# Seven plain chunks and twenty pairs instead of nine and nineteen, with two thirds of the weight sums behind the transforms

## The chip, the cores and the metric

The kernel runs on one core of one Trainium2 chip. The metric is the device time of one execution in microseconds (us). Engines are written as in the profile: PE is TensorE (PEld its weight loads), DVE is VectorE, ACT is ScalarE, POOL is GpSimd, SP is SyncE, which here only issues DMAs.

## What is computed

```python
X = np.fft.rfft(x, axis=1)                 # x: 8 x 3008 x 256
Yr = Xr @ w_r - Xi @ w_i + b_r
Yi = Xr @ w_i + Xi @ w_r + b_i
Y = sign(Y) * maximum(abs(Y) - 0.01, 0)    # on Yr and Yi, the soft threshold
y = np.fft.irfft(Y, n=3008, axis=1)        # 24064 tokens of 256
gate = 1 / (1 + exp(-(y @ w_gate)))        # 256 x 1536
out = (gate * (y @ w_val)) @ w_out         # 1536 x 256
```

Everything is float32. A product of the FFN (and of the mixing by w_r, w_i) is made of three matmuls on rounded high and low parts of its operands, so that a float32 result comes out of the faster matmul type.

## The kernel before

The transforms go batch by batch: a small DFT over 47 (`fwd_d`), a DFT over 64 (`fwd_b`), the complex mixing with the soft threshold (`mix`, 84 calls for batches 1 to 7), and the way back (`inv_b`, then `inv_a`). Between these steps the data go out to HBM and come back. Batch 0 is transformed first, alone. Everything else runs beside the FFN.

The FFN has two forms. **Plain chunks** are 512 tokens wide (`CW`), and there are `NPL` = 9 of them. Each has 12 units `ffn[j]`; a unit is `ffn1` (12 matmuls of 512 columns, a sigmoid, a product, a split into high and low) and `ffn2` of two units earlier (6 matmuls). **Pairs** are 1024 tokens wide, `NPR` = 19 of them; they use a seven-product scheme on 2x2 blocks for both layers, 378 matmuls of 512 columns where two plain chunks have 432. The pairs need sums of weight blocks: `make_t` makes those of the first layer (12 calls, into the DRAM tensor `td`), `make_s` those of the second (6 calls, into `sd`). Both run on POOL and store by POOL's own DMA queue.

Order of work: units 0 to 11 run with the last of the front work. The transforms of batches 1 to 7 are a list `side` of steps with weights; the loop over `j` (units 12 on) issues a unit and then as many steps as the weight per unit allows, such that all but the steps of the last group's inverse (`behind_last`, one `inv_a` a unit) are gone at unit `part`, the last 20 units (`LAST_GAP`) remaining. So in the program before 76 units (12 to 87) lie beside the transforms, then come 20 units with the 16 `inv_a` of the last group, then the pairs. When the transforms are through, their pools are closed and the pool `p4` of the pairs' weights and operands is opened on their memory. A scheduler places the instructions of all these streams on each engine's queue, in an order that is fixed when the program is built.

In the program before, the sums are issued one at each third unit from unit 34 on, all beside the transforms, in buffers that the transforms use too. SP issues nearly all loads and stores in one queue: the loads `vf<-vd` of `inv_a` (two buffers), its stores `yd<-yf`, and, as early as the scheduler finds place for them, the pairs' first weight loads `w1s<-td` and `w2s<-sd` (rings of `NW1` = 4 and `NW2` = 3 buffers in `p4`).

In the pairs the order is written by a planner (`arrange`) with a table of nudges (`NUDGE`); the table, the planner's costs and the pairs' tasks are the same in both programs.

Of the kernel before, what the change touches and what calls it, by code (L numbers as in the profile page):

```python
# [22 lines left out]
LAM = float(np.float32(0.01))  # L23
GROUPS = (1, 1, 2, 2, 2)
CW = 512
NPL = 9
HW = 512
FG = 3
RING, L1_BANKS, L2_BANKS = 6, 3, 2

NF2K, NR2K, NLD, NST, NBIG, NMF, NME, NVF, NVO, NHH, NSG, NYF, NYT = 5, 4, 3, 3, 5, 3, 2, 2, 1, 3, 2, 3, 3
NCB, NTMP, NW1, NW2, NOP = 9, 17, 4, 3, 3
# [208 lines left out]
def tile_fft_mix_ffn(ctx: ExitStack, tc, x, w_r, w_i, b_r, b_i, w_one, w_out, mf, mi, mis, fa, ft, out):  # L241
    nc = tc.nc

    B, D, S = x.shape[0], w_r.shape[0], R1 * R2
    P = 128
    XR = x.shape[2]
    CT = D // P
    NF = w_one.shape[0]
# [7 lines left out]
    NH = NF // 2  # L256
# [23 lines left out]
    def f2k(name):  # L280
        return p2.tile([P, 2, D], F32, tag="f2k", bufs=NF2K, name=name)
# [21 lines left out]
    def big(name):  # L303
        return p2.tile([P, 4, D], F32, tag="big", bufs=NBIG, name=name)
# [126 lines left out]
        held["xs", b, q] = xh, xl  # L431


    def soft(s):
        c = f2k("yc")
        nc.vector.tensor_scalar(c, s, -LAM, LAM, op0=ALU.max, op1=ALU.min)
        sub(c, s, c)  # L437
        return c

    def mix(b, q):  # L440
        xh, xl = held.pop(("xs", b, q))
        pm = bank("pm")
# [12 lines left out]
        c = soft(s)
        yh = r2k("yh")
        yl = r2k("yl")
        nc.scalar.copy(yh, c)  # L458
        sub(yl, c, yh)
        held["ys", b, q] = yh, yl  # L460
# [82 lines left out]
    def result(name):  # L543
        return p3.tile([P, CW], F32, tag="ry", bufs=NYF, name=name)
# [152 lines left out]

    def make_t(fp, i):  # L700
        f0, f1 = 2 * fp, 2 * fp + 1
        g = nc.gpsimd
        b = p2.tile([P, 2, D], F32, tag="st", bufs=NST, name="tb").rearrange("p a (b n) -> p a b n", b=2)
        t = result("tt").rearrange("p (a b n) -> p a b n", a=2, b=2)
        for k, f in enumerate((f0, f1)):
            g.tensor_add(b[:, k], w1h[:, f, i], w1l[:, f, i])
        t = t.rearrange("p a b n -> p (a b) n")
        g.tensor_sub(t[:, 0], b[:, 1, 0], b[:, 0, 0])
        g.tensor_sub(t[:, 2], b[:, 1, 1], b[:, 1, 0])
        g.tensor_add(t[:, 1], t[:, 2], b[:, 0, 0])  # L710
        g.tensor_sub(t[:, 3], b[:, 0, 1], t[:, 1])
        r = p2.tile([P, 4, 2, P], F32R, tag="big", bufs=NBIG, name="tr")
        for k in (0, 2):
            g.tensor_copy(r[:, k:k + 2, 0], t[:, k:k + 2])
            g.tensor_sub(r[:, k:k + 2, 1], t[:, k:k + 2], r[:, k:k + 2, 0])
        g.dma_start(td[fp, i][:, 3:], r.bitcast(F32))
        for v, w in enumerate((w1h, w1l)):
            g.dma_start(td[fp, i][:, 0:2, v], w[:, f0, i].bitcast(F32))
            g.dma_start(td[fp, i][:, 2, v], w[:, f1, i, 1].bitcast(F32))

    def make_s(fp):
        g = nc.gpsimd
        if fp >= NH - FG:
            g.dma_start(pd[fp - NH + FG], w2[:, 2 * fp:2 * fp + 2].bitcast(F32))
        a = p2.tile([P, 2, D], F32, tag="st", bufs=NST, name="sa")
        g.tensor_add(a, w2[:, 2 * fp:2 * fp + 2, 0], w2[:, 2 * fp:2 * fp + 2, 1])
        a11, a21, a12, a22 = a[:, 0, :P], a[:, 0, P:], a[:, 1, :P], a[:, 1, P:]
        w = big("sw").rearrange("p a n -> p (a n)").rearrange("p (k n) -> p k n", n=P)
        zero = w[:, 7]
        g.memset(zero, 0.0)  # L730
        g.tensor_copy(w[:, 0], a11)
        g.tensor_sub(w[:, 1], zero, a12)
        g.tensor_sub(w[:, 3], zero, a22)
        g.tensor_add(w[:, 4], a22, a21)
        g.tensor_sub(w[:, 5], w[:, 4], a11)
        g.tensor_sub(w[:, 6], a11, a21)
        g.tensor_sub(w[:, 2], a12, w[:, 5])
        for k0, k1 in ((0, 4), (4, 7)):
            r = p2.tile([P, 4, 2, P], F32R, tag="big", bufs=NBIG, name="sr")[:, :k1 - k0]
            g.tensor_copy(r[:, :, 0], w[:, k0:k1])  # L740
            g.tensor_sub(r[:, :, 1], w[:, k0:k1], r[:, :, 0])
            g.dma_start(sd[fp // FG, k0:k1, :, fp % FG].rearrange("k p v n -> p k v n"), r.bitcast(F32))
# [22 lines left out]
    def first_operands():  # L765

        y = held["y", 0]
        a11, a21, a12, a22 = y[:, 0, 0], y[:, 0, 1], y[:, 1, 0], y[:, 1, 1]
        s1, s2 = (p4.tile([P, HW], F32, tag=f"{n}0", bufs=1, name=n) for n in ("s1f", "s2f"))
        g = nc.gpsimd  # L770

        def split(name, v):
            t = xs[name] = xop(name)
            nc.scalar.copy(t[:, 0], v)
            sub(t[:, 1], v, t[:, 0])

# [12 lines left out]
        return [sums, lambda: split("s2", s2), lambda: split("a12", a12), lambda: split("s1", s1), s3,
                lambda: split("a22", a22), s4]  # L790
# [702 lines left out]
```

## Time and profile before

| | us |
|---|---|
| median of 3 runs (2697.5 to 2703.36) | 2700.75 |
| the profiled execution, its own time | 2710.75 |
| its span, first to last instruction | 2708.9 |
| units 12 to 87 beside the transforms, from 183.5 to 912.2 | 728.7 |
| the last 20 units, from 912.2 to 1021.2 | 109.0 |
| the 19 pairs, from 1021.2 on | 1687.7 |

Times in the profile are microseconds from the start of the span. Busy times of PE are modelled: matmuls overlap, so the mean time of one matmul (0.39 us) is longer than the step from one to the next. An engine's queue is served in order. A wait that the profile shows on a queue (SPq, POOLq) holds back everything behind it in that queue.

### The profile page before, as it was taken

Reading aid. Unit: us, or ns where it says so; the run is one execution under the profiler, and the core shown is the slowest. Engines: PE = TensorE matmul, PEld = TensorE weight load, DVE = VectorE, ACT = ScalarE, POOL = GpSimd, SP = SyncE. Lnnn points to the kernel's source line nnn. Section 1 sums busy time; section 2 is a strip of 40 time slices with the busy share of each in tenths; the row PEclk is TensorE's granted clock in tenths of the full one; section 3 lists DMA queues with packets and bytes.
Section 4 is the critical chain, followed back from the end, with each engine's and each line's share of the span. In section 5 each row is a group of like instructions: output and inputs, shape, how many; then the busy total and the mean of one; then the engine's idle time right before and its main releaser. Section 6 shows DMA issues by size and latency. Waiting matters only on the chain.

```text
span 2708.9 us, 45080 instructions
## 1 busy us (share of the span) xinstructions
PE 2662.7 (98%) x16763; PEld 2178.5 (80%) x16763; DVE 2140.7 (79%) x3100; ACT 1670.5 (62%) x2852; POOL 1055.0 (39%) x963
## 2 busy tenths in 40 slices
PE   9999999999999999999999999999999999999999
PEld 6778888888888878878788788878788788887877
DVE  5778888687789537888888888888888788888876
ACT  4565554545444446676677766766667667776665
POOL 1441012132235013544555445444554455544532
PEclk9999999999999999999999999999999999999999
DMA  9987655677666675878877888787877788787874
GB/s 294 293 285 197 193 151 168 204 208 208 179 185 179 171 218 164 251 237 251 263 238 246 251 246 265 236 247 237 256 249 242 234 269 239 244 259 243 259 227 135
DMA packets 257659, 617.82 MB, mean 228 GB/s; under 512 B 26464, under 2 KB 130656, under 8 KB 257440
## 3 DMA queue, kind: packets, MB, share of 16 engines
q1 hardware_dynamic: 222720, 521.29, 58.5%
q0 software_dynamic: 34608, 93.60, 16.2%
q8 instruction: 133, 2.18, 0.3%
q14 instruction: 86, 0.70, 0.1%
q10 hardware_dynamic: 112, 0.04, 0.0%
HBM read 440.50 MB, written 116.13 MB: 205 GB/s over the span
## 4 chain that ended last, share of the span: by engine, by line
PE 62%; DMA 14%; DVE 10%; ACT 6%; POOL 4%; issue 3%; SPq 0%; DVEq 0%; POOLq 0%; ACTq 0%
PE z L1155 15%; PE l2z L1155 13%; DMA h<-h 11%; PE c L1155 7%; PE pm L447 4%; PE b L1155 3%; PE pb L413 2%; POOL t L1320 2%; PE pia L524 2%; PE pg L577 2%; ACT op L1331 1%; PE pg L578 1%; POOL h L1320 1%; PE po L605 1%; PE pv L577 1%
## 5 line engine op out<-in xcount | busy, mean ns | idle before, releaser
L1155 PE MATMUL z<-xop,w1s 128*128 128x512 f32 x2592 | 684.3, 391 | 11.4 <-ACT tmp L1246 11.1
L1155 PE MATMUL l2z<-op,w2s 128*128 128x512 f32 x2331 | 599.8, 392 | 3.9 <-DMA w2s<-sd 1.9
L1155 PEld LDWEIGHTS z<-xop,w1s 128*128 128x128 f32 x2592 | 484.9, 188 | 123.8 <-ACT tmp L1246 24.0
L1155 PEld LDWEIGHTS l2z<-op,w2s 128*128 128x128 f32 x2331 | 436.2, 188 | 108.2 <-ACT tmp L1351 7.4
L1246 ACT COPY tmp<-z 128x512 f32<-128x512 f32 x684 | 394.3, 584 | 183.1 <-PE z L1155 175.2
L1333 DVE TENSOR_TENSOR op<-h,op 128x1024 fp32r<-128x1024 f32 (+1 forms) x444 | 472.2, 1078 | 24.9 <-ACT op L1331 19.5
L1331 ACT CAST op<-h 128x1024 fp32r<-128x1024 f32 (+1 forms) x444 | 366.4, 837 | 176.1 <-DMA h<-h 100.1
L1155 PE MATMUL c<-xop,w1s 128*128 128x512 f32 x1296 | 362.1, 392 | 5.1 <-DVE h L1287 3.3
L1293 POOL TENSOR_TENSOR h<-tmp 128x512 f32<-128x512 f32 x114 | 180.1, 1580 | 379.6 <-DVE tmp L1249 362.6
L1155 PEld LDWEIGHTS c<-xop,w1s 128*128 128x128 f32 x1296 | 242.7, 188 | 62.8 <-DVE h L1287 10.5
L1249 DVE TENSOR_TENSOR tmp<-tmp,c 128x512 f32<-128x512 f32 x342 | 231.5, 681 | 62.9 <-ACT tmp L1246 41.2
L1320 POOL TENSOR_TENSOR t<-h 128x512 f32<-128x512 f32 x111 | 173.3, 1562 | 158.0 <-DVE h L1285 158.0
L1265 ACT ACTIVATE tmp<-tmp 128x512 f32<-128x512 f32 x342 | 210.3, 632 | 28.4 <-DVE tmp L1249 28.4
L1314 POOL DMA_DIRECT2D h<-h x148 | 128.3, 900 | 165.8 <-DVE h L1289 56.0
L447 PE MATMUL pm<-w_sb,xsh 128*128 128x256 f32 x1008 | 184.4, 285 | 0.0
L1155 PE MATMUL b<-xop,w1s 128*128 128x512 f32 x648 | 182.3, 390 | 0.0
L447 PEld LDWEIGHTS pm<-w_sb,xsh 128*128 128x128 f32 x1008 | 152.9, 189 | 1.0 <-ACT xsh L429 0.4
L1320 POOL TENSOR_TENSOR h<-h 128x512 f32<-128x512 f32 x111 | 148.9, 1341 | 8.7
L458 ACT CAST yh<-yc 128x512 fp32r<-128x512 f32 x84 | 52.2, 621 | 147.0 <-DVE yc L437 146.9
L1155 PEld LDWEIGHTS b<-xop,w1s 128*128 128x128 f32 x648 | 121.3, 188 | 26.0 <-DVE tmp L1249 0.5
L447 PE MATMUL pm<-w_sb,xsl 128*128 128x256 f32 x504 | 139.6, 277 | 0.0
L585 DVE TENSOR_TENSOR sg<-sg,pv 128x512 f32<-128x512 f32 x108 | 74.1, 686 | 74.2 <-PE pv L579 56.0
(199 smaller groups left out, 4933.0 us busy)
## 6 DMA issues: line engine op xcount, KB each, us to landing
w1s<-td SPq DMA_DIRECT2D x228, 896.0 KB, 6.3
w2s<-sd SPq DMA_DIRECT2D x259, 384.0 KB, 4.3
h<-h POOLq DMA_DIRECT2D x74, 512.0 KB, 6.2
zf<-zd SPq DMA_DIRECT2D x96, 256.0 KB, 3.5
vf<-vd SPq DMA_DIRECT2D x128, 192.0 KB, 4.0
vd<-vz SPq DMA_DIRECT2D x84, 256.0 KB, 2.7
ypair<-yd SPq DMA_DIRECT2D x19, 1024.0 KB, 7.4
out_dram<-acc SPq DMA_DIRECT2D x76, 256.0 KB, 4.3
```

The source lines that it names most:

```text
L447: nc.tensor.matmul(o, l, r, start=(i == 0), stop=(i == len(mms) - 1))
L577: nc.tensor.matmul(t, wh, yth[:, ct], start=(ct == 0), stop=False)
L585: nc.vector.tensor_mul(h, sg, pv)
L1155: nc.tensor.matmul(o, ws[i], vs[j], start=first and not i and not j, stop=i == 1, skip_group_check=not first)
L1246: return t, on("ACT", 0.59, at, lambda: a_.copy(t.get(), z.get()), [z], [t], deps)
L1249: return on("DVE", 0.67, at, lambda: add(t.get(), s.get(), o.get()), [x for x in (s, o) if x is not t], [t], deps)
L1265: return on("ACT", 0.635, at, lambda: a_.activation(t.get(), (o or t).get(), AF.Sigmoid), [o] if o else [], [t], deps)
L1293: made[3, q] = on("POOL", 1.3, 16, lambda: g_.tensor_mul(at_h(3), g22.get(), v.get()), [g22, v], [h], [d22, e22], True)
L1314: return [[on("POOL", 0.9, at + q0, lambda q0=q0, q1=q1: g_.dma_start(h.get()[:, dst, q0:q1], h.get()[:, src, q0:q1], accum_op=ALU.add), [ ...
L1320: return [[on("POOL", 1.3, at + q, lambda q=q: g_.tensor_sub(v()[:, q], h.get()[:, a, q], h.get()[:, b, q]), [h], [o], sum((d[q] for d in ...
L1331: hi = on("ACT", 0.19 + 0.43 * n, at - 8 + q0, lambda q0=q0, q1=q1: a_.copy(t.get()[:, 0, q0:q1], v()[:, q0:q1]), [t_in], [t], sum((d[i] f ...
L1333: lo.append([on("DVE", 0.13 + 0.555 * n, at - 5 + q0, lambda q0=q0, q1=q1: sub(t.get()[:, 1, q0:q1], v()[:, q0:q1], t.get()[:, 0, q0:q1]), ...
```

## The change

- `NPL` goes from 9 to 7, and with it the pairs from 19 to 20. The number of units falls from 108 to 84; units 12 to 63 (52 of them) now carry the same transforms, and the last 20 are units 64 to 83.
- `LATE` = 12: of the 18 sums, six `make_t` are issued beside the transforms, one at each sixth unit. The other six `make_t` and all six `make_s` are issued after the transforms, two a unit from unit 64 on, in `p4`: the sums themselves in the fourth buffer of the ring `w1s` (`room`), their rounded parts in the three buffers of the ring `w2s` (`rounded`).
- The stores of the unsummed weights move out of `make_t` and `make_s` into `store_plain`, one at each third unit from unit 24 on. `make_s` rounds and stores in three pieces instead of two, `make_t` (the late ones) stores in two pieces instead of one.
- `soft`: for odd `q` (42 of 84 calls) the threshold is `min(s + LAM, relu(s - LAM))`, a Relu on ACT and one DVE instruction, instead of two DVE instructions.
- The four sums of the first pair's operands (`first_operands`) move from POOL to DVE.

```diff
-NPL = 9
+NPL = 7
+LATE = 12
 ...
-    def soft(s):
+    def soft(s, by_act=False):
         c = f2k("yc")
+        if by_act:
+            nc.scalar.activation(c, s, AF.Relu, bias=lam)
+            nc.vector.scalar_tensor_tensor(c, s, LAM, c, op0=ALU.add, op1=ALU.min)
+            return c
         nc.vector.tensor_scalar(c, s, -LAM, LAM, op0=ALU.max, op1=ALU.min)
         sub(c, s, c)
 ...
-        c = soft(s)
+        c = soft(s, q % 2 == 1)
 ...
+    def room():
+        return p4.tile([P, 14 * P], F32, tag="w1s3", bufs=1, name="sums")
+    def rounded(n):
+        turns[0] += 1
+        return p4.tile([P, FG, 2, P], F32R, tag=f"w2s{turns[0] % NW2}", bufs=1, name="hilo")[:, :n]
 ...
-        for k0, k1 in ((0, 4), (4, 7)):
-            r = p2.tile([P, 4, 2, P], F32R, tag="big", bufs=NBIG, name="sr")[:, :k1 - k0]
+        for k0, k1 in ((0, 3), (3, 6), (6, 7)):
+            r = rounded(k1 - k0)
 ...
-        g = nc.gpsimd
+        g = nc.vector          # first_operands
 ...
-        if sums and j > 3 * NF - 3 and j % 3 == 1:
+        if len(sums) > LATE and j >= 2 * NF and j % 6 == 0:
+            sums.pop(0)()
+        if plain and j >= 2 * NF and j % 3 == 0:
+            plain.pop(0)()
+        for _ in range(2 if p4 and sums else 0):
             sums.pop(0)()
```

Three places show what becomes of the queues. Line numbers of the changed program are its own (L501 before is L507 there, L536 is L542, L1342 is L1375). A bracket names the semaphores that an instruction waits for: DMASW is a DMA issued by POOL, DMAHW one issued by SP, the others are engines.

The first place is SP's queue in the last 20 units, around the first load of second-layer weights for the pairs (`w2s<-sd`). Before:

```order
L536 DMA yd_104<-yf_12250 128x2x188 [waits DMAHW5_49,Activation_49]
L501 DMA vf_12280<-vd7_99 48x1024 [waits DMAHW6_49,PE_49]
L501 DMA vf_12280<-vd7_99 48x1024 [waits DMAHW7_49]
L1342 DMA w2s_13007<-sd_102 128x768 [waits DMAHW0_49]
L536 DMA yd_104<-yf_12317 128x2x188 [waits DMAHW1_49,Activation_49]
L536 DMA yd_104<-yf_12320 128x2x188 [waits DMAHW2_49,Activation_49]
L501 DMA vf_12358<-vd7_99 48x1024 [waits DMAHW3_49,PE_49]
L501 DMA vf_12358<-vd7_99 48x1024 [waits DMAHW4_49]
```

And in the changed program:

```order
L507 DMA vf_11788<-vd7_99 48x1024 [waits DMAHW7_49,DMAHW0_49,PE_49]
L542 DMA yd_104<-yf_11753 128x2x188 [waits Activation_49]
L542 DMA yd_104<-yf_11756 128x2x188 [waits DMAHW1_49,Activation_49]
L507 DMA vf_11788<-vd7_99 48x1024 [waits DMAHW2_49]
L1375 DMA w2s_12365<-sd_102 128x768 [waits DMASW5_49,DMASW6_49,DMASW4_49,DMASW7_49,DMASW2_49,DMAHW3_49,DMASW1_49,Pool_49]
L1231 DMA ypair_12367<-yd_104 128x2x1024 [waits DMAHW4_49]
L542 DMA yd_104<-yf_11825 128x2x188 [waits DMAHW5_49,Activation_49]
L542 DMA yd_104<-yf_11828 128x2x188 [waits DMAHW6_49,Activation_49]
L507 DMA vf_11860<-vd7_99 48x1024 [waits DMAHW7_49,PE_49]
L507 DMA vf_11860<-vd7_99 48x1024 [waits DMAHW0_49]
```

The load now waits for POOL and for six of POOL's stores, the last of which is that of `hilo_11416`, a part of the last `make_s`. Behind it in the queue stand the loads of the last five `inv_a` (vf_11860 and four more) and the stores of their results.

The second place is POOL's queue where the sums end and the pairs begin. Before, the last `make_s` stands beside the transforms:

```order
L740 CAST sr_11232<-sw_11219 128x3x128
L741 TENSOR_TENSOR sr_11228<-sw_11219,sr_11228 128x4x128 [waits Pool_49]
L741 TENSOR_TENSOR sr_11232<-sw_11219,sr_11232 128x3x128 [waits Pool_49]
L742 DMA sd_102<-sr_11228 128x4x256 [waits Pool_49]
L742 DMA sd_102<-sr_11232 128x3x256 [waits Pool_49]
L778 TENSOR_TENSOR s1f_12545<-ypair_12323 128x512 [waits DMAHW7_49,DMASW2_49]
```

In the changed program, the end of the last sum (ahead of it stand the eleven other late sums, without other work between them):

```order
L766 CAST hilo_11420<-sums_11406 128x3x128 [waits DMASW1_49]
L766 CAST hilo_11416<-sums_11406 128x3x128 [waits DMASW2_49,Pool_49]
L767 TENSOR_TENSOR hilo_11420<-sums_11406,hilo_11420 128x3x128 [waits Pool_49]
L767 TENSOR_TENSOR hilo_11416<-sums_11406,hilo_11416 128x3x128 [waits Pool_49]
L768 DMA sd_102<-hilo_11420 128x3x256 [waits Pool_49]
L768 DMA sd_102<-hilo_11416 128x3x256 [waits Pool_49]
L766 CAST hilo_11424<-sums_11406 128x128 [waits DMASW3_49]
L767 TENSOR_TENSOR hilo_11424<-sums_11406,hilo_11424 128x128 [waits Pool_49]
L768 DMA sd_102<-hilo_11424 128x256 [waits Pool_49]
L1244 TENSOR_TENSOR s1f_12411<-ypair_12367 128x512 [waits DMAHW4_49,DMAHW0_49,DVE_49]
```

The last `make_s` now ends right ahead of the pairs' first POOL instruction. The first late sum (not shown) waits for DVE's last soft threshold of an odd q and for the last mixing matmuls; from there the twelve follow each other on POOL without a break.

The third place is DVE's queue around a soft threshold (`ys` is its input, `yc` its result). Before:

```order
L453 TENSOR_TENSOR ys<-pm_5383,yt 64x256
L454 TENSOR_TENSOR ys<-yt 64x256
L436 TENSOR_SCALAR yc<-ys 128x512
L437 TENSOR_TENSOR yc<-ys,yc 128x512
L585 TENSOR_TENSOR sg<-sg,pv 128x512
```

In the changed program, for an odd q:

```order
L459 TENSOR_TENSOR ys<-pm_5610,yt 64x256
L460 TENSOR_TENSOR ys<-yt 64x256
L440 SCALAR_TENSOR_TENSOR yc<-ys,yc 128x512
L428 TENSOR_TENSOR xsf<-xsf 128x2x128
L455 TENSOR_TENSOR yt<-pm,bias_sb 128x512
```

One instruction has gone, and the one that is left stands right behind the sum that ACT's Relu reads. It is so in 21 of the 42 places; in the other 21 one or two other DVE instructions stand between.

## Rows read from the trace of the kernel before

**Rows 1.** The page's first part: busy time, share of the span and count.
```profile
PE 2662.7 (98%) x16763; PEld 2178.5 (80%) x16763; DVE 2140.7 (79%) x3100; ACT 1670.5 (62%) x2852; POOL 1055.0 (39%) x963
```

**Rows 2.** Busy times by stage: front and units 0 to 11, units 12 to 87 beside the transforms, the last 20 units, the pairs. Columns: stretch, length, busy us (and count) of PE, PEld, DVE, ACT, POOL, granted PE clock, DMA share, GB/s.
```profile
0.00:183.50 183.50, 172.86 (x984) 124.21 (x985) 123.19 (x213) 102.32 (x186) 61.82 (x104) 0.98 0.95 304
183.50:912.20 728.70, 719.61 (x7055) 619.26 (x7055) 602.27 (x1020) 366.88 (x648) 171.78 (x245) 0.99 0.63 184
912.20:1021.20 109.00, 107.06 (x1534) 86.06 (x1526) 36.25 (x50) 45.37 (x89) 7.19 (x5) 0.98 0.71 201
1021.20:2708.90 1687.70, 1663.20 (x7210) 1348.97 (x7208) 1378.99 (x1818) 1155.96 (x1930) 814.22 (x609) 1.00 0.78 240
```

**Rows 3.** The same columns for three stretches beside the transforms, each of 12 mixings.
```profile
290.70:382.50 91.80, 91.80 (x730) 79.44 (x730) 80.14 (x146) 48.80 (x84) 5.39 (x9) 1.00 0.56 158
602.10:720.30 118.20, 117.68 (x1380) 101.05 (x1379) 90.51 (x151) 60.25 (x110) 31.72 (x50) 1.00 0.69 201
818.10:912.20 94.10, 91.77 (x1091) 81.93 (x1092) 84.23 (x136) 43.20 (x79) 35.40 (x44) 1.00 0.55 164
```

**Rows 4.** PE in the last 20 units, in order of time: start, us, instruction, in brackets the idle time before it and what ended it. The second to the eighteenth matmul of a unit, then two parts of one `inv_a` and the next unit.
```profile
982.70 0.40 PE L578 MATMUL pg<-ytl,w1h 128*128 128x512 f32 x1
...
986.34 0.39 PE L607 MATMUL po<-hl,w 128*128 128x512 f32 x1
986.83 0.28 PE L524 MATMUL pia<-ft_sb,vf 48*64 48x47 f32 x2
987.52 1.14 PE L524 MATMUL pia<-ft_sb,vf 48*64 48x47 f32 x62 [0.41 <-DMA vf<-vd]
```

**Rows 5.** One instruction that each pair but the first has once, on POOL: min/median/max ns, first and last start.
```profile
L1216 POOL TENSOR_TENSOR ypair<-ypair x18: 1294/1736/1747, 1026.9 to 2522.4; 128x512 f32<-128x512 f32 x18
```

**Rows 6.** DVE's groups by line beside the transforms (183.5 to 912.2): count, busy us, mean ns of one, idle time before them and what ended it.
```profile
L437 DVE TENSOR_TENSOR yc<-ys,yc 128x512 f32<-128x512 f32 x83 | 62.8, 757 | 2.5
L459 DVE TENSOR_TENSOR yl<-yc,yh 128x512 fp32r<-128x512 f32 x83 | 61.7, 743 | 21.6 <-ACT yh L458 16.5 <-PE pv L579 4.8
L594 DVE TENSOR_TENSOR hl<-sg,hh 128x512 fp32r<-128x512 f32 x77 | 58.3, 757 | 23.2 <-ACT hh L593 22.3
...
L585 DVE TENSOR_TENSOR sg<-sg,pv 128x512 f32<-128x512 f32 x76 | 52.3, 688 | 16.0 <-ACT sg L583 7.5 <-PE pv L579 6.6
L436 DVE TENSOR_SCALAR yc<-ys 128x512 f32<-128x512 f32 x84 | 41.1, 490 | 2.2
```

**Rows 7.** Two groups of the pairs, same columns, over the whole span: the nearest to ACT's Relu and to DVE's new instruction.
```profile
L1265 ACT ACTIVATE tmp<-tmp 128x512 f32<-128x512 f32 x342 | 210.3, 632 | 28.4 <-DVE tmp L1249 28.4
L1287 DVE SCALAR_TENSOR_TENSOR h<-c,tmp 128x512 f32<-128x512 f32 x111 | 76.4, 689 | 2.6
```

**Rows 8.** POOL in order of time: the first and last instruction of a quick and of an ordinary `make_t`, then of a quick and of a slow `make_s`.
```profile
709.70 1.41 POOL L706 TENSOR_TENSOR tb<-w1h,w1l 128x256 f32<-128x256 f32 x2 [35.52 <-DMA vd<-vz]
711.19 0.46 POOL L708 TENSOR_TENSOR tt<-tb 128x128 f32<-128x128 f32 x1
...
716.30 0.57 POOL L716 DMA_DIRECT2D td<-tr  x1 [0.15 <-issue]
...
432.27 1.59 POOL L706 TENSOR_TENSOR tb<-w1h,w1l 128x256 f32<-128x256 f32 x2 [21.42 <-DMA vd<-vz]
...
439.65 0.57 POOL L716 DMA_DIRECT2D td<-tr  x1 [0.31 <-POOL tr L715]
...
782.81 1.44 POOL L726 TENSOR_TENSOR sa<-w 128x512 f32<-128x512 f32 x1 [15.61 <-DMA vd<-vz]
...
792.21 1.54 POOL L742 DMA_DIRECT2D sd<-sr  x2
...
817.81 1.38 POOL L726 TENSOR_TENSOR sa<-w 128x512 f32<-128x512 f32 x1 [23.84 <-DMA vd<-vz]
...
829.26 1.53 POOL L742 DMA_DIRECT2D sd<-sr  x2
```

**Rows 9.** SP's queue in the last 20 units, in order of time.
```profile
964.93 0.92 SPq L501 DMA_DIRECT2D vf<-vd  x2
965.91 0.42 SPq L1342 DMA_DIRECT2D w2s<-sd  x1
```

**Rows 10.** DMA issues: what, queue, count, KB each, median us from issue to landing. The first two are of the last 20 units, the third of the whole span.
```profile
vf<-vd SPq DMA_DIRECT2D x34, 192.0 KB, 4.2
...
w2s<-sd SPq DMA_DIRECT2D x3, 384.0 KB, 4.6
...
sd<-sr POOLq DMA_DIRECT2D x6, 384.0 KB, 5.1
```

**Rows 11.** First and last start of three instructions (min/median/max ns, first and last start): DVE's two last soft thresholds; the `inv_a` matmuls of the last 20 units (starts come in groups some 5.4 us apart); the first product of the pairs.
```profile
L437 DVE TENSOR_TENSOR yc<-ys,yc x2: 691/692/693, 905.1 to 912.2; 128x512 f32<-128x512 f32 x2
...
L524 PE MATMUL pia<-ft_sb,vf x1152: 223/232/253, 919.4 to 1010.0; 48*64 48x47 f32 x192
...
L1155 PE MATMUL c<-s,w1s x72: 389/389/434, 1021.2 to 1102.5; 128*128 128x512 f32 x72
```

**Rows 12.** Before the first plain unit PE waits for a DMA: the wait, and the stages around it (columns as in rows 2; the eighth number is the granted PE clock).
```profile
103.12 2.24 PE L524 MATMUL pia<-ft_sb,vf 48*64 48x47 f32 x64 [3.17 <-DMA vf<-vd]
...
98.00:102.30 4.30, 1.95 (x5) 0.49 (x3) 2.44 (x4) 2.78 (x6) 2.73 (x6) 1.00 0.91 240
102.30:109.10 6.80, 5.98 (x121) 4.97 (x125) 1.01 (x2) 0.85 (x2) 3.41 (x7) 0.50 1.02 370
```

More of the change, by code (lines that the diff above doesn't have):

```diff
@@ L688, in ffn_units, with store_plain @@
         return [lambda n=n: unit(n) for n in range(len(seq))], own(0), own(NPL - 1)[-1] + 1
+    def room():
+        return p4.tile([P, 14 * P], F32, tag="w1s3", bufs=1, name="sums")
+    turns = [0]
+    def rounded(n):
+        turns[0] += 1
+        return p4.tile([P, FG, 2, P], F32R, tag=f"w2s{turns[0] % NW2}", bufs=1, name="hilo")[:, :n]
+    def store_plain(fp, i):
+        for v, w in enumerate((w1h, w1l)):
+            nc.gpsimd.dma_start(td[fp, i][:, 0:2, v], w[:, 2 * fp, i].bitcast(F32))
+            nc.gpsimd.dma_start(td[fp, i][:, 2, v], w[:, 2 * fp + 1, i, 1].bitcast(F32))
+        if i and fp >= NH - FG:
+            nc.gpsimd.dma_start(pd[fp - NH + FG], w2[:, 2 * fp:2 * fp + 2].bitcast(F32))
     def make_t(fp, i):
@@ L702, in make_t @@
         g = nc.gpsimd
-        b = p2.tile([P, 2, D], F32, tag="st", bufs=NST, name="tb").rearrange("p a (b n) -> p a b n", b=2)
-        t = result("tt").rearrange("p (a b n) -> p a b n", a=2, b=2)
+        if p4:
+            b, t = (room_[:, 4 * P * k:4 * P * (k + 1)].rearrange("p (a b n) -> p a b n", a=2, b=2)
+                    for room_ in (room(),) for k in range(2))
+        else:
+            b = p2.tile([P, 2, D], F32, tag="st", bufs=NST, name="tb").rearrange("p a (b n) -> p a b n", b=2)
+            t = result("tt").rearrange("p (a b n) -> p a b n", a=2, b=2)
         for k, f in enumerate((f0, f1)):
@@ L711, in make_t @@
         g.tensor_sub(t[:, 3], b[:, 0, 1], t[:, 1])
-        r = p2.tile([P, 4, 2, P], F32R, tag="big", bufs=NBIG, name="tr")
+        r = None if p4 else p2.tile([P, 4, 2, P], F32R, tag="big", bufs=NBIG, name="tr")
         for k in (0, 2):
[L714 to L719, printed above, removed]
+            o = rounded(2) if p4 else r[:, k:k + 2]
+            g.tensor_copy(o[:, :, 0], t[:, k:k + 2])
+            g.tensor_sub(o[:, :, 1], t[:, k:k + 2], o[:, :, 0])
+            if p4:
+                g.dma_start(td[fp, i][:, 3 + k:5 + k], o.bitcast(F32))
+        if r is not None:
+            g.dma_start(td[fp, i][:, 3:], r.bitcast(F32))
     def make_s(fp):
         g = nc.gpsimd
-        if fp >= NH - FG:
-            g.dma_start(pd[fp - NH + FG], w2[:, 2 * fp:2 * fp + 2].bitcast(F32))
-        a = p2.tile([P, 2, D], F32, tag="st", bufs=NST, name="sa")
+        v = room()
+        a = v[:, 8 * P:12 * P].rearrange("p (f n) -> p f n", f=2)
         g.tensor_add(a, w2[:, 2 * fp:2 * fp + 2, 0], w2[:, 2 * fp:2 * fp + 2, 1])
         a11, a21, a12, a22 = a[:, 0, :P], a[:, 0, P:], a[:, 1, :P], a[:, 1, P:]
-        w = big("sw").rearrange("p a n -> p (a n)").rearrange("p (k n) -> p k n", n=P)
+        w = v[:, :8 * P].rearrange("p (k n) -> p k n", n=P)
         zero = w[:, 7]
@@ L803, in tile_fft_mix_ffn @@
     bias4 = p0.tile([P, D], F32, name="bias4")
-    ebias = cw.tile([P, P], F32, name="ebias")[:, :1]
+    ebias = cw.tile([P, P], F32, name="ebias")
+    ebias, lam = ebias[:, :1], ebias[:, 1:2]
     ft_sb = const.tile([P, P], F32, name="ft_sb")
@@ L904, in tile_fft_mix_ffn @@
     nc.vector.memset(ebias, -896.0 * 2.0 ** 23)
+    nc.vector.memset(lam, -LAM)
     mfs, mis_ = {}, {}
@@ L1048, in tile_fft_mix_ffn @@
     p4 = None
+    plain = [lambda fp=fp, i=i: store_plain(fp, i) for fp in range(NH) for i in range(2)]
     sums = [lambda fp=fp, i=i: make_t(fp, i) for fp in range(NH) for i in range(2)] + [lambda fp=fp: make_s(fp) for fp in range(NH)]
```

## The prediction

> **What bounds the kernel now.** I read four views, from the whole to the place. The page's busy times come first: PE 98% of the span, DVE 79% [rows 1]. Such a share hides stages, so the second view is the busy time by stage [rows 2]. Beside the transforms PE is busy for 719.6 of 728.7 us, DVE for 602.3, POOL for 171.8; in the last 20 units DVE has 36.3 of 109.0 and POOL next to nothing; in the pairs PE has 1663 of 1688. So PE sets the pace in all three, and POOL and DVE lie idle in the last 20 units. The third view cuts the transforms' stage finer [rows 3]: the stretches from 290.7 and from 818.1 have DVE at 80.1 of 91.8 and 84.2 of 94.1 us, almost the second bound. Fourth come the queues in the last 20 units. The reader should see in [rows 4] that an inverse step waits 0.41 us for its load vf<-vd, which has come only just in time, and in [rows 9] that the pairs' first w2s load is issued at 965.9, between the loads and stores of the inverse steps, 55 us before the pairs begin at 1021.2 [rows 11]. Before, that is free: it waits for nothing that is late.
>
> **The change part by part.**
>
> *One more pair.* One instruction a pair starts 18 times from 1026.9 to 2522.4 [rows 5]: 1495.5 / 17 = 88.0 us a pair. Its order, its table and its loads are unchanged, so **+88.0**.
>
> *24 plain units less.* Seventeen instructions of a unit, the second to the eighteenth, start from 982.70 to 986.34 [rows 4]: 3.64 / 16 = 0.2275 us a matmul, 18 of them 4.10 us. As long as PE is the bound beside the transforms, 52 units instead of 76 save 24 x 4.10 = 98.3 us there; the transforms' own matmuls stay. But the transforms' DVE work stays too and is pressed into less time. DVE's work falls by 24 x (0.688 + 0.757) = 34.7 us with the units [rows 6]. A soft threshold costs DVE 0.490 + 0.757 us before [rows 6]; the one instruction after I take from the nearest row, 0.689 [rows 7]. That is 0.56 less, 42 times: 23.4 us. With two thirds of the sums gone from POOL there, DVE gets quicker: the threshold's second instruction takes 0.757 on average, but 0.692 at the end of the stage, where POOL stands still [rows 6, 11]. Three such instructions (L437, L459, L594) have about 0.065 us each to gain, 243 times [rows 6], 15.8 us; two thirds of that are 10. DVE is left with 602 - 35 - 23 - 10 = 534 us for 630, 85% against 83% before. On average PE stays the bound. In the two close stretches DVE had 164.4 of 185.9 us, 88% [rows 3]. They lose 24 x 185.9 / 728.7 = 6.1 units, 25 us of PE's work and 9 of DVE's; the 12 cheaper ones of their 24 thresholds give back 7, and the missing sums some 2. PE would then need 161 us, DVE 146 at the 88% that it reached, 166. That costs 5 us; with a part of the next item I take **-90** in all, and -98 as one end.
>
> *The wait in the cheaper threshold.* ACT's Relu costs 0.632 [rows 7], 42 times 26.5 us on an engine that is busy 367 of 729 [rows 2]: hidden. DVE has to wait for it, and in 21 places with nothing between: 21 x 0.7 (0.632 and a hop) = 15 us of idle time at most, which eats most of the 23 saved. If none of it hides and DVE sets the pace, the other end is -98 + 5 + 15 = -78. Less than nothing it cannot cost, and since DVE had 126 us of idle time in this stage [rows 2], I have put only 3 into the -90.
>
> *Six sums and the plain stores beside the transforms.* These are what POOL did there before, at a slower rate. POOL is busy 172 of 729 us [rows 2]: 0.
>
> *First pair's sums on DVE.* Four instructions of about 0.7 us in a stretch where DVE is busy a third of the time [rows 2]: 0.
>
> *Twelve sums in the last 20 units.* This is the term that decides. POOL is free there, so the sums themselves cost nothing. But their buffers are w2s and w1s3, and SP's first w2s load must wait for the store of the last sum. Behind it in SP's queue stand the loads of the last five inverse steps, and PE cannot pass these. How long do the sums take? A quick `make_t` took 709.70 to 716.87, 7.2 us, an ordinary one 432.27 to 440.22, 8.0; a quick `make_s` 782.81 to 793.75, 10.9, a slow one 817.81 to 830.79, 13.0 [rows 8]. A late `make_t` has one DMA issue more (0.57), a late `make_s` a third piece: one more issue (0.77) and the fixed part of two instructions. Two sizes give that part: 0.46 us for 128 columns and 1.41 / 2 for 256 [rows 8], so 0.22 each. That makes 7.7 to 8.5 and 12.1 to 14.2: twelve sums take 119 to 136 us. All these were measured beside a DVE that was busy for 80 to 90% of the time [rows 3]; in the last units it is busy for a third. If POOL loses beside DVE the share that DVE loses beside POOL (0.692 / 0.757 = 0.91), 119 becomes 109. I take **114**, with 109 and 136 as ends.
>
> The sums start at about the end of the last threshold, 912.9 on the clock of before [rows 11]. The fifth inverse step from the end began at 986.8 [rows 4], 73.9 us later, the last ended at 1010. With the change its load comes after 114 us of sums, 5.1 for the landing of the last store, 2.5 for six issues of 0.42 us on SP, and 4.2 for its own landing [rows 9, 10]: 125.8. So PE stands for 125.8 - 73.9 = **+52**, with 47 and 74 as ends. Nothing covers it: the units behind the step are in PE's queue behind it, and the 34.4 us from there to the pairs come after. The pairs' own loads are late by no more, so nothing is added then.
>
> *PE's clock.* After a wait of 3.17 us PE ran at a granted clock of 0.50 for 6.8 us, the lower of its two levels, 1.2 GHz [rows 12]. A wait of 50 us should do the same once: half of 6.8 is lost at most, **+2**.
>
> Sum: 88 - 90 + 52 + 2 = **+52 us**. The profiled execution took 2710.75 itself (its span 2708.9); it lies 10 us above the median of the runs, 2700.75, to which I add the difference: **2753**.
>
> A rule on the sums' length: the Trainium skill's page SBUF — State Buffer, section "SBUF: two separate sides", says that a VectorE instruction with two SBUF inputs and a GpSimd one that reads SBUF lock each other out for a whole instruction. The rows agree in kind (0.757 against 0.692), and by the rule the late sums would also wait out what DVE does in their first 74 us.
>
> **The rivals.**
>
> 1. *The sums wait for DVE.* DVE is busy 36.3 of 109 us in the last units [rows 2], so 24.6 in the 74 us before PE stops. If POOL stood still in all of that, on top of the 119 of the quick rows, the sums would take 144, and PE would stand for 82: 2753 + 30 = 2783. For it speaks the spread of one kind of sum from 10.9 to 13.0 us; against it that a part of DVE's work reads PSUM and that the 119 hold such waits already.
>
> 2. *DVE becomes the bound beside the transforms.* The wait for ACT takes all that the threshold saves, and the close stretches follow DVE: the stage shrinks by 75 instead of 90, and the time is 2768. For it speaks that the new instruction stands right behind its input in half of the places; against it, that PE kept 91.8 of 91.8 us beside a DVE at 87% [rows 3].
>
> 3. *Faster: SP's queue never stands.* If the last store has landed when SP reaches the load, the term of 52 and the clock's 2 are gone and the rest is 88 - 90, with 98 instead of 90 even -10: 2691 to 2701, in the middle 2698. It decides at the sums' length: to be done in 73.9 - 5.1 - 2.5 - 4.2 = 62 us, a sum would have to take 5.2 on average, where no `make_t` took under 7.1 and no `make_s` under 10.9. It could also be that the change doesn't do what it seems to, if the wait named in the queue were met by an earlier store; but the load writes a buffer that the last sum rounds into.
>
> **How the numbers follow.** Main case 0.65 (2753, by its ends 2753 - 8 - 5 = 2740 to 2753 + 12 + 22 = 2787), first rival 0.12, second 0.13, third 0.10. The range leaves out the third rival, and at the top the case that both far ends meet; below 2740 it keeps 6 us for what the rows don't tell: **2734 to 2785**. A measurement of this kernel can tell 0.2%, 5.4 us, from no change. Half of the third rival's times, 2691 to 2701, lie more than that below 2700.75: faster 0.05, same 0.05, and **slower 0.90**, all other cases.
>
> **What would show it.** In the profile of the changed kernel: the stage beside the transforms ends some 90 us earlier; on SP a wait of about 50 us ahead of the w2s load and none of it before; an idle time of PE ahead of an inverse step (pia), ended by the load vf<-vd, of 47 to 74 us; POOL without a gap from the last threshold on for 109 to 136 us; then 34 us to the pairs, 88 us a pair. It is wrong if PE has no such gap, if POOL's sums are through within 62 us, or if DVE rather than PE is without idle time beside the transforms.

## The result and the profile after

The change makes the kernel slower: 2737.8 us, median of 4 runs (2734.39 to 2740.26), against 2701.07 for the kernel before beside it (2697.5 to 2703.36); ratio 1.0135, 95% interval 1.0119 to 1.0151. The profiled execution took 2734.39 us, span 2732.6.

Of the page after, from the busy times in 40 slices of 68 us (tenths) the rows of PE and POOL, and the granted clock:
```profile
PE   9999999999999399999999999999999999999999
...
POOL 1431111010109525445544455545554455444532
PEclk9999999999999699999999999999999999999999
```
The fourteenth slice is the only one in which PE stands for most of the time, and its granted clock is lower there. The rows by stage (cut after the last soft threshold and at the first pair; columns as in [rows 2]) say what moved:
```profile
0.00:183.50 183.50, 173.34 (x985) 124.36 (x986) 123.74 (x214) 103.08 (x186) 61.67 (x104) 0.98 0.95 305
183.50:817.00 633.50, 620.29 (x6626) 538.97 (x6625) 516.95 (x923) 363.72 (x640) 63.39 (x89) 1.00 0.69 199
817.00:976.10 159.10, 109.31 (x1513) 88.42 (x1513) 40.52 (x53) 44.08 (x87) 105.23 (x181) 0.83 0.62 190
976.10:2732.60 1756.50, 1739.55 (x7588) 1420.21 (x7586) 1449.10 (x1914) 1216.91 (x2032) 858.15 (x642) 1.00 0.79 243
```
Against [rows 2] the stretch beside the transforms is 95.2 us shorter, the last 20 units are 50.1 longer, the pairs 68.8 longer: +23.7, and so much lie the two profiled spans apart. (The medians lie 36.7 apart; on the pairs more below.) In the third row PE's busy time has hardly grown: the 50 us are a stop.

PE in that stage, in order of time (start, us, instruction, the idle time before it and what ended it):
```profile
893.75 0.39 PE L613 MATMUL po<-hl,w 128*128 128x512 f32 x1
939.98 0.41 PE L530 MATMUL pia<-ft_sb,vf 48*64 48x47 f32 x2 [45.84 <-DMA vf<-vd]
```
The releaser is a load. Whether that load was slow or late is not in this row; it is in SP's queue, in order of time:
```profile
883.83 0.47 SPq L507 DMA_DIRECT2D vf<-vd  x1
930.90 0.34 SPq L1375 DMA_DIRECT2D w2s<-sd  x1
931.29 0.43 SPq L1231 DMA_DIRECT2D ypair<-yd  x1
931.82 0.92 SPq L542 DMA_DIRECT2D yd<-yf  x2
932.84 1.04 SPq L507 DMA_DIRECT2D vf<-vd  x2
```
and in what SP waited for over the stage (us in total, times, longest):
```profile
SPq L1375 <- DMA sd<-hilo: 46.3, 1, 46.3
```
SP stood for 46.3 us at the w2s load, for the store of a late sum, and issued the next load of an inverse step 49 us after the one before. POOL's queue shows the sums that it waited for, the first instruction of the first one, the first of each `make_s`, and the last store:
```profile
817.79 1.86 POOL L732 TENSOR_TENSOR sums<-w1h,w1l 128x256 f32<-128x256 f32 x2 [122.12 <-DVE yc L440]
...
866.32 1.28 POOL L752 TENSOR_TENSOR sums<-w 128x512 f32<-128x512 f32 x1
...
877.61 1.29 POOL L752 TENSOR_TENSOR sums<-w 128x512 f32<-128x512 f32 x1
...
888.40 1.28 POOL L752 TENSOR_TENSOR sums<-w 128x512 f32<-128x512 f32 x1
...
899.00 1.27 POOL L752 TENSOR_TENSOR sums<-w 128x512 f32<-128x512 f32 x1
...
909.19 1.27 POOL L752 TENSOR_TENSOR sums<-w 128x512 f32<-128x512 f32 x1
...
919.37 1.27 POOL L752 TENSOR_TENSOR sums<-w 128x512 f32<-128x512 f32 x1
...
928.97 0.58 POOL L768 DMA_DIRECT2D sd<-hilo  x1 [0.30 <-POOL hilo L767]
```
The twelve sums run from 817.79 to 929.55, 111.8 us, without a wait of more than 2.0 us. They answer to [rows 8].

### The profile page after: what moved, and what is told of

It is laid out like the page before. It is cut to its first block, busy times and chain, and to the rows that moved or that the text cites. A ratio compares the mean times of both kernels' runs of the same rounds, so it can differ in the third digit from the quotient of the medians.

```text
span 2732.6 us, 45175 instructions
## 1 busy us (share of the span) xinstructions
PE 2642.5 (97%) x16709; PEld 2172.0 (79%) x16709; DVE 2130.3 (78%) x3102; ACT 1727.8 (63%) x2944; POOL 1088.4 (40%) x1016
## 4 chain that ended last, share of the span: by engine, by line
PE 68%; DVE 9%; DMA 8%; POOL 7%; ACT 5%; issue 2%; SPq 0%; POOLq 0%; DVEq 0%; ACTq 0%
PE z L1188 18%; PE l2z L1188 16%; PE c L1188 9%; DMA h<-h 6%; PE pm L453 4%; PE b L1188 4%; PE pb L414 2%; POOL t L1353 2%; ACT op L1364 1%; PE pia L530 1%; PE pa L314 1%; PE pg L583 1%; DVE op L1366 1%; PE po L611 1%; PE po L612 1%
## 5 line engine op out<-in xcount | busy, mean ns | idle before, releaser
L1188 PE MATMUL z<-xop,w1s 128*128 128x512 f32 x2736 | 720.3, 391 | 5.8 <-ACT tmp L1279 5.7
L1188 PE MATMUL l2z<-op,w2s 128*128 128x512 f32 x2457 | 627.1, 390 | 1.4 <-DMA w2s<-sd 1.1
L1188 PEld LDWEIGHTS z<-xop,w1s 128*128 128x128 f32 x2736 | 512.3, 188 | 120.7 <-ACT tmp L1279 15.3
L1188 PEld LDWEIGHTS l2z<-op,w2s 128*128 128x128 f32 x2457 | 459.6, 188 | 104.2 <-ACT tmp L1384 3.5
L1279 ACT COPY tmp<-z 128x512 f32<-128x512 f32 x720 | 415.8, 585 | 191.1 <-PE z L1188 183.5
L1366 DVE TENSOR_TENSOR op<-h,op 128x1024 fp32r<-128x1024 f32 (+1 forms) x468 | 496.4, 1075 | 23.4 <-ACT op L1364 17.2
L1364 ACT CAST op<-h 128x1024 fp32r<-128x1024 f32 (+1 forms) x468 | 386.3, 838 | 168.3 <-DMA h<-h 91.1
L1188 PE MATMUL c<-xop,w1s 128*128 128x512 f32 x1368 | 381.8, 392 | 5.3 <-DVE h L1320 3.6
L1188 PEld LDWEIGHTS c<-xop,w1s 128*128 128x128 f32 x1368 | 256.1, 188 | 65.9 <-DVE h L1320 11.2
L732 POOL TENSOR_TENSOR tb<-w1h,w1l 128x256 f32<-128x256 f32 x12 | 11.3, 956 | 360.6 <-DMA vd<-vz 257.0
L591 DVE TENSOR_TENSOR sg<-sg,pv 128x512 f32<-128x512 f32 x84 | 57.7, 687 | 124.4 <-ACT sg L589 70.1
```

Of the source, the lines that this page charges most:

```text
L591: nc.vector.tensor_mul(h, sg, pv)
L1188: nc.tensor.matmul(o, ws[i], vs[j], start=first and not i and not j, stop=i == 1, skip_group_check=not first)
L1279: return t, on("ACT", 0.59, at, lambda: a_.copy(t.get(), z.get()), [z], [t], deps)
L1364: hi = on("ACT", 0.19 + 0.43 * n, at - 8 + q0, lambda q0=q0, q1=q1: a_.copy(t.get()[:, 0, q0:q1], v()[:, q0:q1]), [t_in], [t], sum((d[i] f ...
L1366: lo.append([on("DVE", 0.13 + 0.555 * n, at - 5 + q0, lambda q0=q0, q1=q1: sub(t.get()[:, 1, q0:q1], v()[:, q0:q1], t.get()[:, 0, q0:q1]), ...
```

## The experiments

The theory: SP's first load for the pairs waits for the last sum, and the loads of the inverse steps wait behind it in the same queue. The rivals: the inverse steps wait for POOL, for the sums' bytes or for the clock; or the time is lost to DVE.

**1. Six late sums instead of twelve.**
```diff
-LATE = 12
+LATE = 6
-        if len(sums) > LATE and j >= 2 * NF and j % 6 == 0:
+        if len(sums) > LATE and j >= 2 * NF and j % 3 == 0:
```


> The changed kernel with six of the twelve late sums put back beside the transforms (all make_t there, at each third unit of the last two thirds; only the six make_s behind it). Theory of the queue (SP's first w2s load waits for the last late sum, the loads of five inverse steps wait behind it): six make_s take about 63 us instead of 111.8, so the last sum ends about 880 and SP comes free before PE wants what stands behind; the PE gap of 45.8 us shrinks to 0 to 5 us, six more sums beside the transforms cost 0 to 6 us there; 2690 to 2700 us, faster than the kernel before. Rival (the sums' place costs by contention with DVE or by the clock, and the gap has another cause): the gap stays above 30 us and the time above 2720 us.

Measured: 2734.07 us, ratio to before 1.011 (1.0086 to 1.0134): a miss for the time, and for the gap, which shrank to 14.8 us where 0 to 5 were expected:
```profile
PE pia L530 <- DMA vf<-vd: 15.5, 3, 14.8
```
The six `make_s` took 67.8 us, 846.2 to 914.0, 5 more than expected. But the stretch beside the transforms, here to 845.0, grew:
```profile
183.50:845.00 661.50, 637.82 (x6620) 546.81 (x6619) 523.85 (x921) 362.38 (x638) 103.66 (x154) 0.98 0.67 195
```
That is 28 us more than the 633.5 above for the same matmuls: 10.5 of it idle time of PE (661.50 - 637.82 against 13.2), 17.5 busy time, at a granted clock of 0.98 instead of 1.00. The waits of PE that a DMA ended grew from 1.7 to 8.9 us. One place, around an inverse step and a wait for zf<-zd:
```profile
660.00:665.00 5.00, 3.34 (x72) 2.34 (x71) 2.61 (x5) 2.83 (x6) 1.57 (x2) 0.85 0.59 185
665.00:670.00 5.00, 5.00 (x16) 4.13 (x16) 0.00 (x0) 0.96 (x2) 0.00 (x0) 0.50 0.94 262
670.00:675.00 5.00, 1.22 (x9) 0.91 (x7) 1.65 (x2) 1.42 (x2) 4.19 (x8) 0.84 1.06 250
675.00:680.00 5.00, 4.79 (x15) 4.19 (x16) 1.19 (x2) 1.56 (x3) 1.01 (x2) 0.50 1.05 295
```
After each short stop (660 to 665, 670 to 675) PE runs at a granted clock of 0.50, the lower of its two levels, for some microseconds. Only the place of six sums differs, so what the smaller gap gave (the last units are 29.6 us shorter) was paid there. What of a sum delays the loads was not separated; the DMA engines are full (0.94 to 1.06) in the last three of these rows.

**2. Twelve late sums, and the loads that wait for them in POOL's queue.**
```diff
-            ins = [on("SP", 0.45, at - 16, lambda: nc.sync.dma_start(w.get().bitcast(F32), sd[gi, r]), [], [w], lat=1.25)]
+            ins = [on("SP", 0.45, at - 16, lambda: (g_ if g == 0 and r in FIRST else nc.sync).dma_start(w.get().bitcast(F32), sd[gi, r]), [], [w], lat=1.25)]
...
-                           lambda: nc.sync.dma_start(t.get().bitcast(F32), td[k // 2 % NH, k % 2]), writes=[t], lat=2.7)
+                           lambda: (g_ if k == NW1 - 1 else nc.sync).dma_start(t.get().bitcast(F32), td[k // 2 % NH, k % 2]), writes=[t], lat=2.7)
```
(FIRST = (0, 1, 4).)

> The changed kernel with the sums where they are, but the loads that wait for a late sum (the first three w2s loads and the last w1s load) issued from GpSimd's queue behind the sums instead of from SyncE's. Theory of the queue: SP never stands, the loads of the inverse steps land in time, the PE gap of 45.8 us ahead of pia goes and the dip of the clock with it; 2737.8 - 45.8 - 2.3 = about 2690 us (2686 to 2696). Rival (inverse steps wait for the bytes of the sums, or for GpSimd, and not for the queue): a gap of 30 us or more stays and the time stays above 2720 us.

Measured: 2688.73 us, 0.9937 (0.9918 to 0.9955) of before, so it beats both kernels. PE's longest wait for vf is 0.7 us, and the stage has 114.2 us instead of 159.1, with the sums as long as ever (POOL 105.5):
```profile
PE pia L531 <- DMA vf<-vd: 1.6, 3, 0.7
...
820.00:934.20 114.20, 110.70 (x1515) 89.43 (x1514) 40.02 (x53) 44.61 (x88) 105.51 (x179) 0.94 0.76 241
```
Same sums, same bytes, other queue, no stop: the theory holds and the first rival is out. The dip of the clock did not go with the stop, though that was expected: the stage's granted clock is 0.94, where the kernel before has 0.98.

**3. Only the w2s loads moved** (the first of the two edits of experiment 2).

> As the kernel with four loads moved, but only the three w2s loads leave SyncE's queue; the w1s load that reads the last late sum stays there, about two inverse steps (10.9 us) later in SP's order. Theory of the queue: any one load in it that waits for the last sum is enough to hold what stands behind; the gap of 45.8 us shrinks by the work that is now ahead of the stop, to about 35 us, and the time is about 2727 us. Rival (only the w2s loads hold): about 2690 us, as with four loads moved.

Measured: 2727.35 us, 1.0085 (1.0065 to 1.0105). PE's waits for loads in that stage, and SP's:
```profile
PE pia L531 <- DMA vf<-vd: 39.5, 7, 35.5
```
```profile
SPq L1221 <- POOL hilo L768: 38.2, 1, 38.2
```
The gap is 35.5 us as expected: one waiting load is enough, and what counts is how much work stands ahead of it in the queue: PE comes to the stop 11.1 us later (one inverse step further) and goes on only 0.8 later.

**4. Experiment 2 with every threshold on DVE.**
```diff
-        c = soft(s, q % 2 == 1)
+        c = soft(s)
```


> As the kernel with four loads moved, with the soft threshold of every mix on VectorE alone, as in the kernel before. It prices the ScalarE half of the threshold without the gap. The forecast took +0 to 15 us for ScalarE's Relu on the path; the stretch beside the transforms came out at 633.5 us, 5 us less than forecast, with TensorE busy 620.3 of it, so the threshold there should be worth little: 2688 to 2698 us (0 to 8 us slower than with it, as VectorE gets some 0.5 us more for each of the odd mixes). Rival (VectorE bounds the stretch once 24 units are gone): 2705 us or more.

Measured: 2691.02 us, 0.9949 (0.993 to 0.9969), against 0.9937 with it. The stage ends 2.6 us later (822.6 against 820.0); DVE is busy 536.8 of 639.1 us there instead of 518.4 of 636.5. By the medians the threshold is worth 2.3 us, which the intervals do not tell from nothing. DVE's 18.4 us of added work cost the stretch 2.6 us, so DVE was not the bound.

**5. The chunks alone.**
```diff
-NPL = 9
+NPL = 7
-        if sums and j > 3 * NF - 3 and j % 3 == 1:
+        if sums and j >= 2 * NF and j % 2 == 0:
```


> The kernel before with only the number of plain chunks changed (seven and twenty pairs); all eighteen sums stay beside the transforms, at each second unit from the 24th on, and the threshold stays on VectorE. It asks whether the late sums are needed for the shorter stretch. One pair adds 87 to 88 us; 24 units less take 80 to 98 us from the stretch beside the transforms. If TensorE still sets the pace there: 2700.9 + 87.5 - 95 = about 2693 us (2690 to 2700). If the sums and the thresholds crowd VectorE and GpSimd in the shorter stretch: the stretch shrinks by 80 us or less, 2708 us or more.

Measured: 2715.9 us, 1.0041 (1.0026 to 1.0056). The stretch beside the transforms, with all eighteen sums in it:
```profile
183.50:849.00 665.50, 637.85 (x6661) 548.54 (x6662) 557.21 (x962) 336.01 (x599) 169.96 (x244) 0.98 0.70 202
```
It shrinks by 63 us, not by 95: the second case of the expectation. DVE is busy for 84% (557.2 of 665.5), against 83% before, so it does not set the pace throughout; as in experiment 1 it is PE's idle time (27.7 us against 9.1 before) and its clock. The crowding that the expectation named has a part in it: of PE's waits in this stretch DVE ended 13.9 us (3.3 before), DMAs 7.7 (none before). The longest kinds are
```profile
PE pb L413 <- DMA zf<-zd: 6.3, 2, 5.1
PE pi L484 <- ACT yh L458: 4.2, 6, 1.3
PE pd L360 <- DVE ys L453: 3.0, 4, 1.4
PE pi L485 <- DVE yl L459: 2.8, 4, 0.9
```
Experiment 4 has late sums and no cheaper threshold, and its stretch is 639.1 us long. So the late sums make most of what the stretch is shorter, and their waiting load is what takes it back. (Six sums more cost the stretch 28 us in experiment 1, twelve more 26 to 32 here; why the price does not go with their number is open.)

**6. The threshold alone, on the kernel before.**
```diff
-        c = soft(s)
+        c = soft(s, q % 2 == 1)
```
(with `soft` and its constant as in the change.)

> The kernel before with only the threshold's change: half of the soft thresholds with ScalarE's Relu and one VectorE operation. TensorE is the bound of the stretch beside the transforms, so no change: 2697 to 2704 us. If ScalarE's Relu comes onto the path (it waits behind ScalarE's evictions): up to 2716 us.

Measured: 2705.32 us, with the kernel before at 2703.48 beside it, 1.0008 (0.9994 to 1.0022): no change.

**7. The kernel before, profiled once more.**

> The kernel before, profiled once more, to size the pair term. The profiled execution that the forecast rests on took 2708.9 us against a median of 2700.8, and its pairs took 88.0 us each (87.2 to 91.4); those of the changed kernel's took 86.9 with the same order of instructions on each engine. If that difference is one of executions, pairs of this one take 87.0 to 87.5 us at a time near 2701; if it belongs to the kernel, 88.0 again.

Measured: one run, 2709.7 us, pairs 88.17 us each (1498.9 / 17 by the instruction of [rows 5]): about 88.0 again. In the profiles, then, 19 pairs are slower each than 20. In the stretch 1100 to 2500 of both kernels (about 16 pairs) PE has one kind of wait that differs clearly, first before, then after:
```profile
PE z L1155 <- ACT tmp L1246: 10.0, 21, 2.2
```
```profile
PE z L1188 <- ACT tmp L1279: 3.6, 15, 0.3
```
and ACT waits longer for the DMA h<-h, again before and after:
```profile
ACT op L1331 <- DMA h<-h: 89.3, 49, 4.1
```
```profile
ACT op L1364 <- DMA h<-h: 76.0, 48, 2.8
```
PE's 6.4 us are 0.4 a pair, less than half of the difference. The order of instructions of DVE, ACT and POOL in the pairs is the same.

**8. and 9. Experiment 2 with nine and with eleven chunks.**
```diff
-NPL = 7
+NPL = 9   # 11 in the other
```


> The kernel with four loads on GpSimd's queue, but with nine plain chunks and nineteen pairs as in the kernel before: late sums, split thresholds and the moved loads without the change of chunks. Two questions. What the chunks are worth once nothing else differs: 24 units hold 24 x 18 products of 226.5 ns, 98 us of TensorE, against one pair of 87: about 2688.7 + 98 - 87 = 2700 us if pairs cost the same. And what the pairs' period goes with: in the profiles it is 87.7 to 88.2 us with nine chunks and 86.7 to 87.0 with seven, by the same order of instructions. If it goes with the number of chunks, it is about 87.9 here and the profiled span near 2712; if it goes with the late sums or the thresholds, 86.9 and 2698.

> As the kernel with four loads moved and nine chunks, with eleven chunks and eighteen pairs: the same exchange once more in the other direction. TensorE alone: 2688.7 + 2 x (98 - 87) = 2711 us. If the pairs' period goes with the number of chunks, it is 87.5 or more here as well; if nine chunks are a case of their own, 86.9.

Measured: 2695.93 us, 0.9986 (0.9974 to 0.9999), with nine; 2689.45 us, 0.996 (0.9947 to 0.9972), with eleven. Nine come out below the 2698 to 2712 of the expectation. The stretch beside the transforms with nine chunks:
```profile
183.50:898.50 715.00, 711.11 (x6994) 614.10 (x6993) 556.64 (x978) 396.33 (x688) 59.39 (x89) 1.00 0.62 175
```
Eleven miss the expected 2711 by far: 24 units cost less than their matmuls' 98 us. From seven to nine chunks the rows show why: PE is idle for 3.9 us of this longer stretch and for 12.6 of the shorter one of experiment 2 (623.95 of 636.50), and the granted clock is 1.00 and 0.99 in the stretch and the last units here, 0.99 and 0.94 there. The first pair starts at 934.2, 1013.6 and 1101.9 with seven, nine and eleven chunks, so 24 units cost 79 and 88 us, about a pair. With the queue free the three times lie within 7.2 us. A pair takes 86.75, 87.49 and 86.83 us in these three profiles: nine chunks, with 19 pairs, are a case of their own, whether the sums are late (87.5) or not (87.6 to 88.2).

**10. and 11. The rows of yd longer by 4 KB,** in the kernel before and in experiment 2:
```diff
-    yd = tc.dram_tile([CT, P, B * S - T0], F32, name="yd").rearrange("t p n -> p t n")
+    yd = tc.dram_tile([CT, P, B * S - T0 + 2 * HW], F32, name="yd").rearrange("t p n -> p t n")
```


> The kernel before with each row of the scratch tensor yd in HBM (it hands the sequence columns of the pairs from the transforms to the pairs) 1024 elements longer; no instruction is added or removed. The profiles show pairs of 87.8 us with 19 pairs and of 86.9 to 87.1 with 18 and 20, by the same order. The only thing in the pairs that the number changes is where data lies: a row of yd has 19, 20 or 18 times 4 KB. If the layout of yd is the cause, pairs here take 86.9 to 87.1 us and the time falls by 10 to 17 us, to 2686 to 2694 us. If it is not, 87.8 and no change: 2697 to 2706 us.

> The kernel with four loads on GpSimd's queue and seven chunks, with the same 1024 elements more in each row of yd (21 times 4 KB for its 20 pairs). If an odd multiple of 4 KB is what makes pairs slow, they take 87.6 us or more here and the time rises by 14 to 20 us from 2688.7, to 2703 to 2709 us. If the layout of yd has no part in it: 86.9 us and 2684 to 2693 us.

Measured: 2698.4 us, 0.9997 (0.9985 to 1.0009), pairs 87.64 us; and 2688.42 us, 0.9951 (0.9938 to 0.9965), pairs 86.86. The length of yd's rows has no part in it. Why 19 pairs cost more each stays open.

## Why the prediction was right, and where its sizes were off

The range held the time and the likeliest case was the one that came; the prediction was 15 us too high, most of it by the term for one more pair.

- **+52, SP's queue: right, and shown.** Measured 45.8, just under the lower end of 47. The steps, from the first sum to PE's restart:
  - The sums took 111.8 us, for 114 forecast. A `make_t` took 8.1 us on average (7.7 to 8.5 forecast), a `make_s` 10.5 (12.1 to 14.2, or 11.0 with the share of 0.91).
  - SP's w2s load went out 1.35 us after the end of the last sum (929.55), where the forecast had 5.1 for a landing. The store that the load waits for, that of `hilo_11416`, is not the last one: it is the second of the two issued from 926.33 to 927.83, and the median of these stores from issue to landing is 3.0 us in this profile.
  - From there to the inverse step (939.98) it took 9.1 us, for 6.7 forecast.
  - PE had reached that step 76.35 us after the first sum had begun, not 73.9. So 111.8 + 1.35 + 9.1 - 76.35 = 45.9, the 45.8 but for rounding.

  The gap stands ahead of the fifth inverse step from the end, and 36 us lie from there to the pairs (34 forecast). Experiments 2 and 3 take it away whole and in part.
- **The rule on the sums' length.** With DVE at work (7.1 of 22.1 us) two `make_s` took 11.3 and 10.8 us; with DVE idle, the last three (from 899.00) took 10.2 each, by the rows of POOL. Single instructions are longer by half a microsecond in the first two, the copy of L757 once 0.81 us against 0.29. This agrees in kind with the Trainium skill's page SBUF — State Buffer, section "SBUF: two separate sides" (PE and most transfers stand still in those three too, so DVE is not singled out), but over a whole sum the size is a tenth at most, no standstill: rival 1 had 144 us for the sums and 2783.
- **-90, 24 units less: measured -95.2** against the profile of before and -88.5 against that of experiment 10 (722.0, below), both between the ends. But it was put down to the units almost alone, so the close fit is in part luck. With the sums left beside the transforms these give 63 (experiment 5). The forecast let the moved sums count through DVE's speed only, 10 us of its time; what they cost is stops of PE and its clock after them, and the more so the shorter the stretch: moving them (with the thresholds) gives 7 to 14 us with nine chunks (722.0 to 728.7 without, 715.0 with, experiment 8), 32 with seven (665.5 to 633.5). Some 6 of these come back in the last units even where nothing stands (109.0 to 115.1 with nine, 108.5 to 114.2 with seven). Rival 2 is out: PE is busy for 620.3 of 633.5 us and DVE for 517.0, where the forecast had 534, and the threshold is worth nothing that can be told (experiments 4, 6). DVE did wait 16.9 us for ACT's Relu, more than the 15 that the forecast had at most, but it had the time.
- **+2, the clock: 2.3,** (1 - 0.54) x 5 us, an estimate from the first of these rows. The granted clock is still at its lower level when PE is at work again:
```profile
940.00:945.00 5.00, 4.62 (x70) 3.96 (x71) 0.69 (x1) 1.47 (x3) 0.00 (x0) 0.54 1.00 280
945.00:950.00 5.00, 5.00 (x81) 3.95 (x80) 1.38 (x2) 2.06 (x4) 0.00 (x0) 1.00 0.61 185
```
- **+88.0, one more pair: mis-sized.** This is the term that failed: "its order, its table and its loads are unchanged" was taken to mean that the other pairs stay as long. The pairs' stage grew by 68.8 us between the two profiles, since all 20 pairs take 86.9 us (from the same instruction of each pair, after and before in [rows 5]):
```profile
L1249 POOL TENSOR_TENSOR ypair<-ypair x19: 1287/1735/1748, 982.2 to 2546.1; 128x512 f32<-128x512 f32 x19
```
That is 1563.9 / 18 = 86.88 against 87.97. Of the 28.3 us between the forecast +52 and the profiles' 23.7 this term makes 19.2; the stretch makes 5.2, the last units 3.9 (54 forecast with the clock, 50.1 measured). Between the medians the difference is smaller. The profile of experiment 10 is one of the same instructions in an execution of 2698.1 us, near the median; its rows from the stretch beside the transforms on:
```profile
183.50:905.50 722.00, 712.48 (x7051) 615.51 (x7051) 600.82 (x1020) 365.18 (x645) 173.13 (x243) 1.00 0.64 185
905.50:1014.60 109.10, 107.85 (x1530) 86.70 (x1522) 36.23 (x50) 45.45 (x89) 7.17 (x5) 0.97 0.69 201
1014.60:2696.30 1681.70, 1659.19 (x7210) 1346.57 (x7208) 1382.62 (x1818) 1156.10 (x1930) 813.66 (x609) 1.00 0.79 241
```
Against these the stretch is 88.5 us shorter, the last units are 50.0 and the pairs 74.8 longer: +36.3, where the medians lie 36.7 apart. So of the some 15 us that the forecast was too high the pair term makes 13.2, the last units make 4.0, and the stretch takes back 1.5.
- **The step to the median.** The sum was added to the median, 2700.75, though each of its terms came from an execution 10 us above it. Against experiment 10 that execution is 6.7 us longer in the stretch and 6.0 in the pairs. It made the pair term only a little larger, 88.0 a pair for 87.6; that the other 19 pairs became shorter is the larger part.
- **Rival 3 (faster, SP never stands)** was priced at 2691 to 2701; experiment 2, where SP does not stand for a sum, gives 2688.7.

## What to carry to other kernels

When work is moved later, look for the first DMA that waits for it, and then at what stands behind that DMA in its queue: a load nobody needs yet can hold one that is needed at once. Give such a load a queue in which nothing urgent follows it; here that alone turned 1.0135 into 0.9937. And when a stage that is bound by PE is made shorter, count what else is in it: here the same sums cost the stretch 7 to 14 us with nine plain chunks and about 30 with seven.

## What was not expected of the hardware

Short stops of PE cost more than their length beside the transforms: in experiment 1, 10.5 us of added idle time came with 17.5 us of added busy time, and the lower granted clock, as (1 - clock) x 5 us summed over slices, accounts for about 13 of these, an estimate. And pairs with the same order of instructions took 87.5 to 88.2 us in five profiles of kernels with 19 pairs, 86.6 to 87.0 in eight with 18 or 20. With them goes ACT's wait for the DMA h<-h, 87.6 to 93.2 us between 1100 and 2500 in the five, 76.0 to 80.7 in the eight; the cause is open.
